# Sliding-window attention and a SiLU MLP: scores in bands of 192 keys from the second group on, in fp32 too, and one tile for the parts of P

## The chip, the cores and the metric

The kernel runs on one core of a Trainium2 chip. The metric is the device time of one execution in microseconds. The kernel before takes 897.84 us, the median of three runs from 897.73 to 897.88.

## The reference

```python
def _attn_ref(q, k, v):                      # 8 batches, 8 heads, 576 tokens, 64 per head
    scores = scale * np.matmul(q, k.transpose(0, 1, 3, 2))
    rel = pos[:, None] - pos[None, :]
    mask = (rel >= 0) & (rel < window)       # window = 128
    scores = np.where(mask, scores + bias[None], -1000000000.0)   # bias = -slope(head) * |rel|
    attn = np.exp(scores - np.max(scores, axis=-1, keepdims=True))
    attn = attn / (np.sum(attn, axis=-1, keepdims=True) + 1e-09)
    return np.matmul(attn, v)

def reference(...):
    x = attn_out.transpose(0, 2, 1, 3).reshape(4608, 512)
    h = x @ w_in                             # 512 x 2048
    g = h * (1.0 / (1.0 + np.exp(-h)))
    return g @ w_out                         # 2048 x 512
```

A query sees itself and the 127 keys in front of it. All inputs and the output are fp32.

## The kernel before

**Attention.** The 4608 tokens are 36 blocks of 128 rows, nine to each pair of batches (a block of index 4 or 5 in such a nine has two batches in it). A *pair* p is half a block: block i = p // 2 and four of its heads (q = p % 2), so there are 72 pairs. In a pair two indices run over the heads: h, the head in the upper or lower 64 partitions of q and k (D = 64), and u, the two such couples. Each pair passes these steps, one function each:

- `scores` (L535, or `scores_banded`, L556): q times k on TensorE into two PSUM banks `sp`, one for each h.
- `other_batch` (L570 to L577): memsets of what belongs to the other batch, on VectorE.
- `row_max` (L588, L598): adds the bias table `tab` (bf16, one table of 256 columns for each head) and finds each row's extreme, on VectorE, four instructions.
- `exps` (L613): exp with the row's extreme as bias, on ScalarE.
- `p_hi`, `p_lo`: P as two fp16 parts: the high part is ScalarE's (L634, L638), the low part VectorE's (L647, L204) or GpSimd's (L202).
- `p_transpose` (L664, L668): DMA transposes, issued by SyncE, into `hl`.
- `attend` (L713): P times v in 24 fp16 matmuls into one PSUM bank `av`, then `normalize` (L726 to L742), `x_hi`, `x_lo` and a transpose to `xt`. Pairs 0 to 7 do this in another way, by transposes on TensorE (L678) and a copy (L687).

A block of queries needs the keys of its own block and of the one before: 256 keys for 128 queries. That is what pairs 0 to 35 compute: `sp[h][:, u]` is 128 x 256, from fp32 q and k, in two matmuls of 128 columns for each u and h (one, where the block is the first of its nine: pairs 18 and 19). Pairs from 36 on are *banded*: the first 64 queries need keys -128 to 63, the second 64 need -64 to 127, so each half of queries takes 192 keys of its own. There the matmuls are on tiles of 64 rows and 64 columns, with q and k as fp16 high and low parts and three terms. For these pairs the first 64 partitions and the second 64 of the bias table are aligned by `rescale_bias` (L371), which at the third and fourth pair of batches moves and scales the table in two instructions, one for each half of the partitions:

```python
for s in range(2):
    off = HALF * s if b == QK16 else 0
    nc.vector.tensor_scalar_mul(tab[halves[s], :, :WIN], tab[halves[s], :, off : off + WIN], ratio[halves[s]])
```

**P's parts.** Pairs 8 to 35 take two tiles `hr` of the pool tag "hr" (two buffers), one for each u, and issue a transpose (128 x 1024) as soon as one u's parts are in. Pairs from 36 on share one persistent tile, `room[0]` (named hr0_0, 64 + 2048 columns, its gaps zeroed once by `clear_room` on GpSimd at position 150): the second half of queries lies 64 columns further left than the first, and two transposes of 64 partitions x 2048 bring the pair into place.

**The MLP.** Nine groups g of 512 tokens, 16 steps n of 128 features each: gemm1 (L1032, L1037; three passes of fp32r in the first group, fp16 later), the activation (`gt` L1065 on ScalarE, `h` L1071 on VectorE, `gh` or `gb` on ScalarE, `gl` L204 or `gb` L1120 on VectorE) and gemm2 (L1248). In the last groups sums of w_in's and w_out's rows shorten the products (L975, L1151).

**What sets the order.** All engines' instructions are issued in program order, written by hand. The program walks through *positions*, one for each half of a gemm step, and `put(point, fn, *a)` enters a function at a position; `at(p)` is the position of pair p's scores: every 8 positions for pairs 0 to 7, the list `CLOSE` for pairs 8 to 15 (which run beside the first group's MLP), every 7 from pair 18 on. At one position, works stand by rank (`rank_of`). PSUM tag "a" has two banks, which scores and av share.

Of the kernel before, what the change touches and what calls it, by code (L numbers as in the profile page):

```python
# [6 lines left out]
F32 = mybir.dt.float32  # L7
# [11 lines left out]
P = 128  # L19
# [55 lines left out]
SUMS, SUMS_STEP = 200, 28  # L75
IN_GAP = 17
HI_SUM, HI_IN = 1, 1
IN_SUMS = tuple(SUMS + SUMS_STEP * j + IN_GAP for j in range(8))
# [3 lines left out]
ALONE_LATE = 4  # L82
X7, X8, X9 = 448, 455, 462
X_SUMS = {(NG - 2, 1): X7, (NG - 1, 0): X8, (NG - 1, 1): X9}
WIN = P + HALF
HR_TAG = "w1_2"
HL_TAG = "w1_3"
ATTEND_BAND = 18
ATTEND_END = 13
HR_CLEAR = 150  # L90
# [5 lines left out]
POOL_FROM = 116  # L96
# [9 lines left out]
ACT_LOW = 1  # L106
V_HI, V_LO = 10, 6
# [10 lines left out]
SUM_TAGS = tuple(f"w1_{k}" for k in range(7, 15))  # L118
# [18 lines left out]
CLOSE = (-6, 5, 8, 14, 20, 26, 32, 38)  # L137
# [15 lines left out]
def tile_window_attention_then_silu_mlp(ctx, tc, qk, v, w_in, w_out, distance, out):  # L153
# [361 lines left out]
    def banded(p):  # L515
        return p >= 2 * QK16 * NBLK
# [24 lines left out]
    def scores_banded(p, flat):  # L541
# [6 lines left out]
        for u in range(2):  # L548
            for both in (first, second):
                for n, (a, b) in enumerate(((0, 0), (1, 0), (0, 1))):  # L550
                    for s, k, keys, at4 in both:
                        if block_of(i) == 0 and k < i:
                            continue
                        for h in range(2):
                            rows = slice(h * D, (h + 1) * D)
                            nc.tensor.matmul(  # L556
                                sp[h][halves[s], u, at4 : at4 + keys.stop - keys.start],
                                q16[i][rows, a, 2 * q + u, halves[s]], k16[k][rows, b, 2 * q + u, keys],
                                start=n == 0, stop=n == 2, skip_group_check=True,
                            )  # L560
# [18 lines left out]
    def row_max(p, k):  # L579
# [4 lines left out]
        if banded(p):  # L584
            for u in range(2):
                if u not in st[p]["t"]:
                    st[p]["t"][u] = pool.tile([P, 2, WIN], F32, tag="t", bufs=3, name=f"t{p}_{u}")
# [6 lines left out]
        for u, h in [(k, 0), (k, 1)] if p < 2 * GT else [(0, k), (1, k)]:  # L594
            if u not in st[p]["t"]:
                tag, bufs = ("x", 4) if 2 * GT < p < 4 * GT and p % 2 and u else ("t", 3)
                st[p]["t"][u] = pool.tile([P, 2, 2 * P], F32, tag=tag, bufs=bufs, name=f"t{p}_{u}")
# [19 lines left out]
    def clear_room():  # L617
        room[0] = r = pool.tile([P, HALF + 16 * P], F16, tag=HR_TAG, bufs=1, name="hr0_0")
# [4 lines left out]
    def split_of(p, u, what):  # L623
        if banded(p):
# [1055 lines left out]
```

## Time and profile before

| | |
|---|---|
| median of three runs | 897.84 us |
| the profiled execution | 896.72 us |
| its span | 894.9 us |
| busy: PE (TensorE) | 886.3 us, 99% |
| busy: DVE (VectorE), ACT (ScalarE), POOL (GpSimd) | 647.4, 589.1, 418.5 us |
| granted TensorE clock | 1.00 in all stretches |

A profile is one execution, with each instruction's start and duration on its engine. PE is the matmuls, PEld the weight loads, which overlap them, SPq SyncE's queue, which issues DMAs. Lnnn is a line of the kernel. A pipelined matmul's row contains its drain, so rows overlap: what an instruction costs its engine is read from the start of one to the start of the next.

### The profile page before, as it was taken

The numbers are of one execution on the slowest core, as the hardware profiler recorded it, in microseconds if no ns is written. First come the engines' busy times: TensorE is split into PE (matmuls) and PEld (weight loads), VectorE is DVE, ScalarE is ACT, GpSimd is POOL, SyncE is SP. The second block draws the span as 40 slices with busy tenths as digits, with TensorE's granted clock in tenths as the row PEclk, the third lists the DMA queues.
The fourth block names the chain that finished last, engine by engine and source line by source line (L and its number), as shares of the span: only waits on it lengthen the run. The fifth ranks groups of instructions, "written<-read, shape, count | busy, mean of one in ns | idle before, by whom it ended". The sixth has DMA issues, their size and how long they took to land.

```text
span 894.9 us, 22095 instructions
## 1 busy us (share of the span) xinstructions
PE 886.3 (99%) x8617; PEld 589.6 (66%) x8617; DVE 647.4 (72%) x1654; ACT 589.1 (66%) x1321; POOL 418.5 (47%) x494
## 2 busy tenths in 40 slices
PE   9999999999999999999999999999999999999998
PEld 7877777888855555445455554445555568899997
DVE  6997988678876766655777667575776659776665
ACT  7789987776578855777765555565566554465653
POOL 2356651112112211666676776686777412443441
PEclk9999999999999999999999999999999999999999
DMA  8979925345588744869885557565575455400000
GB/s 322 399 191 263 244 56 134 72 95 96 117 216 220 191 96 119 179 163 225 188 155 108 109 105 154 123 118 109 125 166 95 84 85 142 142 26 13 14 25 26
DMA packets 207193, 123.22 MB, mean 138 GB/s; under 512 B 170864, under 2 KB 173040, under 8 KB 207088
## 3 DMA queue, kind: packets, MB, share of 16 engines
q1 hardware_dynamic: 206656, 121.41, 56.7%
q8 instruction: 68, 1.11, 0.5%
q10 hardware_dynamic: 432, 0.39, 0.1%
q14 instruction: 37, 0.30, 0.1%
HBM read 66.72 MB, written 13.63 MB: 90 GB/s over the span
## 4 chain that ended last, share of the span: by engine, by line
PE 79%; DVE 8%; ACT 5%; DMA 3%; POOL 3%; issue 2%; SPq 1%; DVEq 0%; POOLq 0%; ACTq 0%
PE o L1248 26%; PE h L1032 22%; PE m L1151 7%; PE h L1037 5%; PE sp L535 4%; PE av L713 4%; PE h L975 3%; PE hb L975 3%; PE sp L556 2%; PE av L699 1%; ACT t L613 1%; DMA qs<-qk 1%; SPq L664 1%; DMA vm<-v 1%; PE pt L678 1%
## 5 line engine op out<-in xcount | busy, mean ns | idle before, releaser
L1032 PE MATMUL h<-xt,w 128*128 128x512 f16 (+1 forms) x1344 | 269.0, 349 | 0.0
L1248 PE MATMUL o<-w,gb 128*128 128x512 f16 x960 | 224.4, 379 | 0.8 <-DVE gb L1120 0.6
L1032 PEld LDWEIGHTS <-w 128*128 128x128 f16 x1344 | 126.6, 98 | 111.7 <-issue 3.3
L1071 DVE SCALAR_TENSOR_TENSOR h<-gt,h 128x512 f32<-128x512 f32 x112 | 77.6, 693 | 127.2 <-ACT gt L1065 126.6
L1248 PEld LDWEIGHTS <-gb 128*128 128x128 f16 x960 | 90.2, 98 | 104.9 <-DVE gb L1120 2.6
L1065 ACT ACTIVATE gt<-h,tsc 128x512 f32<-128x512 f32 x104 | 71.1, 683 | 112.7 <-PE h L1032 105.2
L202 POOL TENSOR_TENSOR hr<-t,hr 128x384 f16<-128x384 f32 (+2 forms) x54 | 55.9, 1036 | 127.7 <-ACT hr L634 64.4
L202 POOL TENSOR_TENSOR x<-xs,x 128x256 f16<-128x256 f32 x54 | 37.3, 690 | 160.3 <-ACT x L752 151.1
L1248 PE MATMUL o<-w,gh 128*128 128x512 f32 x256 | 82.9, 405 | 0.1
L1106 ACT ACTIVATE gb<-h 128x512 f16<-128x512 f32 x80 | 47.4, 592 | 35.5 <-DVE h L1071 35.2
L613 ACT ACTIVATE t<-t,mx,vsc 128x192 f32<-128x192 f32 x144 | 69.0, 537 | 1.2
L1120 DVE SCALAR_TENSOR_TENSOR gb<-h,gb 128x512 f16<-128x512 f32 x80 | 54.8, 685 | 18.7 <-ACT gb L1106 18.6
L613 ACT ACTIVATE t<-t,mx 128x256 f32<-128x256 f32 (+1 forms) x144 | 61.8, 488 | 3.6 <-DVE mx L598 2.7
L713 PEld LDWEIGHTS <-hl 128*128 128x128 f16 x1464 | 51.8, 98 | 14.6 <-issue 3.9
L713 PE MATMUL av<-v,hl 128*128 128x65 f16 (+1 forms) x1464 | 54.9, 193 | 0.1
L1083 POOL TENSOR_TENSOR gt<-gt 128x256 f32<-128x256 f32 x27 | 21.4, 794 | 68.5 <-DVE gt L1074 68.5
L1248 PEld LDWEIGHTS o<-w,gh 128*128 128x128 f32 x256 | 45.6, 188 | 10.0 <-issue 0.5
L598 DVE CUSTOM_DVE_ANT_0 t<-sp,tab 128x256 f32<-128x256 f32 (+1 forms) x144 | 50.1, 402 | 1.9 <-PE sp L535 1.7
L1248 PE MATMUL o<-w,gl 128*128 128x512 f32 x128 | 50.7, 396 | 0.2
L980 ACT COPY hs<-h 128x128 f32<-128x128 f32 x72 | 19.0, 264 | 41.7 <-PE h L975 38.9
L204 DVE SCALAR_TENSOR_TENSOR hr<-t,hr 128x384 f16<-128x384 f32 (+2 forms) x54 | 42.8, 792 | 5.0 <-ACT hr L634 3.8
L202 POOL TENSOR_TENSOR w<-wm,w 128x512 fp32r<-128x512 f32 x32 | 43.7, 1366 | 2.5
(236 smaller groups left out, 1835.2 us busy)
## 6 DMA issues: line engine op xcount, KB each, us to landing
qs<-qk SPq DMA_DIRECT2D x18, 512.0 KB, 4.6
r<-qk SPq DMA_DIRECT2D x18, 512.0 KB, 4.5
wr<-w_in SPq DMA_DIRECT2D x16, 512.0 KB, 6.5
wr<-w_out SPq DMA_DIRECT2D x16, 512.0 KB, 6.2
rv<-v SPq DMA_DIRECT2D x30, 256.0 KB, 3.6
out<-ot SPq DMA_DIRECT2D x28, 256.0 KB, 2.4
vm<-v SPq DMA_DIRECT2D x27, 256.0 KB, 4.4
q<-qk SPq DMA_DIRECT2D x18, 256.0 KB, 3.4
```

Of the source, the lines that this page charges most:

```text
L202: engine.tensor_sub(out, a, b)
L598: nc.vector.tensor_tensor_reduce(out=st[p]["t"][u][:, h, 2 * P - n :], in0=st[p]["sp"][h][:, u, o].rearrange("p o c -> p (o c)"), in1=tab[ ...
L613: nc.scalar.activation(x, x, AF.Exp, bias=mx[:, 2 * u + h : 2 * u + h + 1], scale=scale)
L713: nc.tensor.matmul(av[:, 2 * u + h, : rhs.shape[-1]], lhs, rhs, start=(n == 0), stop=(n == len(seq) - 1), skip_group_check=True,)
L975: nc.tensor.matmul(h[to], w_of(j, w, a, cc), x_of(g, t, x, b, cc), start=w in ("11", "S1") and i == 0, stop=i == len(terms) - 1, skip_grou ...
L1032: nc.tensor.matmul(o, w[:, wp, cc], x, start=start and k == 0, stop=stop, skip_group_check=True)
L1065: nc.scalar.activation(gt, hps[n], AF.Tanh, scale=scale)
L1071: nc.vector.scalar_tensor_tensor(out=h, in0=gt, scalar=1.0, in1=h, op0=ALU.add, op1=ALU.mult)
L1106: nc.scalar.activation(gh, gt, AF.Copy, scale=cut_of(n))
L1120: nc.vector.scalar_tensor_tensor(out=gl, in0=gt, scalar=cut_of(n), in1=f32(gh) if n // NF < OUT16 else gh, op0=ALU.mult, op1=ALU.subtract)
L1151: nc.tensor.matmul(product(k), a[:, k], sum_part(k, j, part), start=j == 0 and side == 0 and a is gh and part == 0, stop=n == last and a i ...
L1248: nc.tensor.matmul(ops[ti], a[:, t], w, start=(f == 0 and i == 0), stop=(f == NF - 1 and i == len(seq) - 1), skip_group_check=True,)
```

## The change

- `banded` holds from pair 8 on. Pairs 8 to 35 keep fp32 q and k and one term: 16 matmuls (8 of 128 columns, 8 of 64) instead of 8 of 128; pairs 18 and 19 get 8 instead of 4. Row max, exps and parts of these pairs have 192 columns for each head instead of 256.
- `shift_bias`, new, aligns the second half of the bias table once, at position -16, so `rescale_bias` is one instruction.
- All pairs from 8 on use the one room, cleared at position -18; `p_transpose` is called once for a pair, when both u are in. gemm1's sums `hsum` become one tile of the tag "hr".
- Positions and tags move: pairs 10 to 13 one or two positions later (`CLOSE`), av8, av9 and av10 to 15 at 17, 13 and 14 behind their scores (before 17, 12, 15), pair 8's parts at position 4, v's conversion one position later, sums of w_out's rows from 172 in steps of 25 (before 200 and 28), constants of the last groups by one or two (`X8`, `X9`, `POOL_FROM`, `ALONE_LATE`).

The core of the diff:

```diff
-SUMS, SUMS_STEP = 200, 28
-IN_GAP = 17
+SUMS, SUMS_STEP = 172, 25
+IN_GAP, IN_ONE = 16, 131
-HR_CLEAR = 150
+HR_CLEAR = -18
+SHIFT = -16
-POOL_FROM = 116
+POOL_FROM = 114
-CLOSE = (-6, 5, 8, 14, 20, 26, 32, 38)
+CLOSE = (-6, 5, 10, 15, 21, 27, 32, 38)
+LATE9, LATE10 = 0, 0
+P8 = (4, 4)
+A8, A9, A10 = 17, 13, 14
...
-        for s in range(2):
-            off = HALF * s if b == QK16 else 0
-            nc.vector.tensor_scalar_mul(
-                tab[halves[s], :, :WIN], tab[halves[s], :, off : off + WIN], ratio[halves[s]]
-            )
+        nc.vector.tensor_scalar_mul(tab[:, :, :WIN], tab[:, :, :WIN], ratio)
+
+    def shift_bias():
+        nc.vector.tensor_copy(tab[halves[1], :, :WIN], tab[halves[1], :, HALF:])
...
     def banded(p):
-        return p >= 2 * QK16 * NBLK
+        return p >= 2 * GT
...
-                for n, (a, b) in enumerate(((0, 0), (1, 0), (0, 1))):
+                terms = ((0, 0), (1, 0), (0, 1)) if i >= QK16 * NBLK else ((None, None),)
+                for n, (a, b) in enumerate(terms):
                     for s, k, keys, at4 in both:
...
+                            lhs = qs[i][rows, 2 * q + u, halves[s]] if a is None else q16[i][rows, a, 2 * q + u, halves[s]]
+                            rhs = ks[k][rows, 2 * q + u, keys] if a is None else k16[k][rows, b, 2 * q + u, keys]
...
-    def p_transpose(p, u):
...
-        nc.sync.dma_start_transpose(hl[:, : 4 * n], hr[:, : 4 * n * P])
+    def p_transpose(p):
+        tag, bufs = ("hl", 2)
+        if ATTEND_BAND > 12 and p >= LONG_FROM and p % 3 == 2:
+            tag, bufs = HL_TAGS.get(p, HL_TAG), 1
+        both = pool.tile([P, 2, 8, P], F16, tag=tag, bufs=bufs, name=f"hl{p}")
+        st[p]["hl"] = {u: both[:, u] for u in range(2)}
+        for s in range(2):
+            off = HALF * (1 - s)
+            nc.sync.dma_start_transpose(
+                both.rearrange("p u a c -> p (u a) c")[:, :, halves[s]], room[0][halves[s], off : off + 16 * P]
+            )
...
-            late = 2 * (p == 2 * GT + 2)
+            late = {2 * GT + 1: LATE9, 2 * GT + 2: LATE10}.get(p, 0)
...
-                put(n + 4 + late + u * (1 + more), p_transpose, p, u)
+            put(n + 5 + late + more, p_transpose, p)
```

Where the order of instructions changes:

On TensorE, the scores of pair 10 (`sp10`) against gemm2 of the first group (`o0`) and av8. Before:

```order
L1037 MATMUL h2_776<-xh_71,w0_2_648 128x512
L535 MATMUL sp10_0_799<-k4_387,q5_499 128x128
L535 MATMUL sp10_1_800<-k4_387,q5_499 128x128
...
L1248 MATMUL o0_3_751<-w1_1_697,gl1_739 128x512
L1037 MATMUL h3_859<-xh_71,w0_3_745 128x512
L1037 MATMUL h3_859<-xl_72,w0_3_745 128x512
L1037 MATMUL h3_859<-xh_71,w0_3_745 128x512 x2
L1037 MATMUL h3_859<-xl_72,w0_3_745 128x512
L1037 MATMUL h3_859<-xh_71,w0_3_745 128x512
L713 LDWEIGHTS hl8_765
```

and in the change:

```order
L1238 MATMUL o0_3_774<-w1_1_709,gl1_762 128x512
L563 MATMUL sp10_0_849<-k4_387,q5_499 64x128
L563 MATMUL sp10_1_850<-k4_387,q5_499 64x128
L563 MATMUL sp10_0_849<-k5_501,q5_499 64x128
L563 MATMUL sp10_1_850<-k5_501,q5_499 64x128
L563 MATMUL sp10_0_849<-k5_501,q5_499 64x64
...
L1026 MATMUL h3_871<-xh_71,w0_3_768 128x512
L1026 MATMUL h3_871<-xl_72,w0_3_768 128x512
L1026 MATMUL h3_871<-xh_71,w0_3_768 128x512 x2
L1026 MATMUL h3_871<-xl_72,w0_3_768 128x512
L1026 MATMUL h3_871<-xh_71,w0_3_768 128x512
L700 LDWEIGHTS hl8_727
```

Between pair 10's scores and av8 there stood twelve matmuls of gemm2 and six of gemm1, and now six of gemm1 alone.

On VectorE, at the same place, pair 10's row max (`t10`), pair 9's low parts (`hr` from `t9`), `wm4` and `gl2`. Before:

```order
L577 MEMSET sp10_1_800 128x2x64
L598 ISA t10_0_830,mx10_809<-sp10_0_799,tab_67 128x256
L598 ISA mx10_809 128x1
...
L647 SCALAR_TENSOR_TENSOR hr9_0_813<-t9_0_757,hr9_0_813 128x512
L1296 SCALAR_TENSOR_TENSOR wm4_0_825<-wm4_0_825,wr4_0_392 128x512
L204 SCALAR_TENSOR_TENSOR gl2_837<-h2_776,gh2_836 128x512
L647 SCALAR_TENSOR_TENSOR hr9_1_839<-t9_1_759,hr9_1_839 128x512
```

and in the change:

```order
L642 SCALAR_TENSOR_TENSOR hr0_0_528<-t9_0_780,hr0_0_528 128x2x192
L1286 SCALAR_TENSOR_TENSOR wm4_0_831<-wm4_0_831,wr4_0_392 128x512
L209 SCALAR_TENSOR_TENSOR gl2_835<-h2_794,gh2_834 128x512
L576 MEMSET sp10_0_849 64x2x64
L576 MEMSET sp10_1_850 64x2x64
L595 ISA t10_0_883,mx10_867<-sp10_0_849,tab_67 128x192
...
L642 SCALAR_TENSOR_TENSOR hr0_0_528<-t9_1_782,hr0_0_528 128x2x192
```

Pair 9's first low part, `wm4` and `gl2` stood behind the row max and now stand ahead of it.

On VectorE, the place of `shift_bias` (L377 COPY) in the change, where nothing stood before between `hl7` and the next row of `vmx0`:

```order
L271 TENSOR_REDUCE vmx0_523<-early2_230 128x1
L675 COPY hl7_536<-pt7_1_538 128x512
L377 COPY tab_67<-tab_67 64x8x192
L271 TENSOR_REDUCE vmx0_523<-early3_278 128x1
L713 TENSOR_SCALAR r6_557<-av6_547 128x4
```

The four rows around the copy have kept their order.

## Rows read from the trace of the kernel before

**Rows 1.** The page, parts 1 and 4; TensorE's waits: us, times, longest.

```profile
PE 886.3 (99%) x8617; PEld 589.6 (66%) x8617; DVE 647.4 (72%) x1654; ACT 589.1 (66%) x1321; POOL 418.5 (47%) x494
...
PE 79%; DVE 8%; ACT 5%; DMA 3%; POOL 3%; issue 2%; SPq 1%; DVEq 0%; POOLq 0%; ACTq 0%
...
PE warm L224 <- POOL ident masks.py:199: 1.3, 1, 1.3
...
PE pt L678 <- ACT t L613: 0.3, 1, 0.3
```

**Rows 2.** Timeline of TensorE around a pair's scores: start us, us, instruction.

```profile
285.75 0.59 PE L1032 MATMUL h<-xt,w 128*128 128x512 f16 x2
286.27 1.16 PE L535 MATMUL sp<-k,q 64*128 64x128 f32 x16
287.36 0.82 PE L1032 MATMUL h<-xt,w 128*128 128x512 f16 x3
```

**Rows 3.** Lines L535 and L556: ns of one, min/median/max, first and last start.

```profile
L535 PEld LDWEIGHTS sp<-k,q x544: 182/188/188, 4.8 to 342.9; 64*128 64x128 f32 x182
L535 PE MATMUL sp<-k,q x544: 272/272/373, 4.8 to 343.0; 64*128 64x128 f32 x182
...
L556 PEld LDWEIGHTS <-packed x1632: 102/107/110, 354.4 to 728.4; 64*64 64x64 f16 x182
```

**Rows 4.** Timeline of TensorE around a pair of the later groups.

```profile
481.67 1.03 PE L1032 MATMUL h<-xt,w 128*128 128x512 f16 x4
482.62 0.24 PE L556 MATMUL sp<-packed 64*64 64x128 f16 x2
482.63 0.24 PE L556 MATMUL sp<-packed,packed 64*64 64x128 f16 x2
...
482.82 0.19 PE L556 MATMUL sp<-packed 64*64 64x64 f16 x2
...
482.91 0.22 PE L556 MATMUL sp<-packed,packed 64*64 64x128 f16 x2
...
483.27 1.04 PE L1032 MATMUL h<-xt,w 128*128 128x512 f16 x4
```

**Rows 5.** Groups by line and form on ScalarE: busy us, mean ns | idle before.

```profile
L634 ACT CAST hr<-t 128x384 f16<-128x384 f32 x72 | 34.5, 502 | 8.0 <-DMA hl<-hr 7.9
L638 ACT ACTIVATE hr<-t 128x512 f16<-128x512 f32 x52 | 31.4, 620 | 2.1 <-DMA hl<-hr 2.1
```

**Rows 6.** Busy us (instructions) from 75 to 85 us: PE, PEld, DVE, ACT, POOL; clock, DMA.

```profile
75.00:85.00 10.00, 10.00 (x75) 7.91 (x74) 7.76 (x21) 10.00 (x27) 5.83 (x7) 1.00 1.07 269
```

**Rows 7.** Timelines of VectorE and of TensorE near 33 us; line L371.

```profile
33.33 0.42 DVE L742 TENSOR_TENSOR early<-av,r 128x256 f32<-128x256 f32 x1
...
32.65 1.81 PE L767 MATMUL xp<-ident,early 128*128 128x128 f32 x15
...
L371 DVE TENSOR_SCALAR tab<-tab,vsc x4: 607/792/1419, 352.7 to 546.7; 64x1536 bf16<-64x1536 bf16 x4
```

**Rows 8.** Timelines of VectorE, then of TensorE, 53 to 60 us.

```profile
53.37 0.42 DVE L598 CUSTOM_DVE_ANT_0 t<-sp,tab 128x256 f32<-128x256 f32 x1
...
55.61 0.68 DVE L204 SCALAR_TENSOR_TENSOR gl<-h,gh 128x512 fp32r<-128x512 f32 x1
...
54.11 0.90 PE L713 MATMUL av<-v,hl 128*128 128x65 f16 x24
...
56.78 0.39 PE L1248 MATMUL o<-w,gl 128*128 128x512 f32 x1
...
59.16 1.28 PE L535 MATMUL sp<-k,q 64*128 64x128 f32 x14
```

**Rows 9.** SyncE near 449 us, landings of L664, ScalarE near 60 us.

```profile
449.49 3.21 SPq L664 DMA_TRANSPOSE hl<-hr  x2
...
DMA to landing us min/median/max: 3.6/4.2/5.8
...
60.48 0.63 ACT L638 ACTIVATE hr<-t 128x512 f16<-128x512 f32 x1
```

More of the change, by code (lines that the diff above doesn't have):

```diff
@@ L105 @@
 ACT_LATE = 6
-ACT_LOW = 1
-V_HI, V_LO = 10, 6
+ACT_LOW = 2
+SUM_LATE = 2
+V_HI, V_LO = 9, 5
 IN_HI16, IN_LO16 = (9, 8), (6, 4)
@@ L617, in clear_room @@
     def clear_room():
-        room[0] = r = pool.tile([P, HALF + 16 * P], F16, tag=HR_TAG, bufs=1, name="hr0_0")
+        room[0] = r = pool.tile([P, HALF + 16 * P], F16, tag="hr", bufs=1, name="hr0_0")
         gaps = r[:, : 16 * P].rearrange("p (a c) -> p a c", a=8)
@@ L621, in clear_room, with split_of @@
         nc.gpsimd.memset(r[:, 16 * P :], 0.0)
-    def split_of(p, u, what):
-        if banded(p):
-            parts = what[:, HALF:].rearrange("p (u a h c) -> p u a h c", u=2, a=2, h=2)
-            return parts[:, u, :, :, :WIN]
-        n = 2 - blocks(p).start
-        return what[:, : 4 * n * P].rearrange("p (a h c) -> p a h c", a=2, h=2)
-    def p_hi(p, u):
-        t, n = st[p]["t"][u], (2 - blocks(p).start) * P
-        if banded(p):
-            st[p]["hr", u] = hr = room[0]
-            nc.scalar.copy(split_of(p, u, hr)[:, 0], t)
-            return
-        st[p]["hr", u] = hr = pool.tile([P, 8 * P], F16, tag="hr", bufs=2, name=f"hr{p}_{u}")
+    def split_of(u):
+        parts = room[0][:, HALF:].rearrange("p (u a h c) -> p u a h c", u=2, a=2, h=2)
+        return parts[:, u, :, :, :WIN]
@@ L646, in p_lo @@
             return
         nc.vector.scalar_tensor_tensor(
-            out=hr[:, 1], in0=t[:, :, 2 * P - n :], scalar=PSCALE, in1=hr[:, 0], op0=ALU.mult, op1=ALU.subtract
+            out=hr[:, 1], in0=t, scalar=PSCALE, in1=hr[:, 0], op0=ALU.mult, op1=ALU.subtract
         )
-    def p_transpose(p, u):
-        n = 2 - blocks(p).start
-        hr = st[p].pop(("hr", u))
-        if u == 0:
-            tag, bufs = (HL_TAG, 1) if banded(p) and p % 3 == 2 and ATTEND_BAND > 12 else ("hl", 2)
-            st[p]["both"] = pool.tile([P, 2, 8, P], F16, tag=tag, bufs=bufs, name=f"hl{p}")
-        both = st[p]["both"]
-        st[p]["hl"][u] = hl = both[:, u]
-        if banded(p):
-            if u == 0:
-                return
-            for s in range(2):
-                off = HALF * (1 - s)
-                nc.sync.dma_start_transpose(
-                    both.rearrange("p u a c -> p (u a) c")[:, :, halves[s]], hr[halves[s], off : off + 16 * P]
-                )
-            return
-        nc.sync.dma_start_transpose(hl[:, : 4 * n], hr[:, : 4 * n * P])
+    def p_transpose(p):
[9 more added lines that the diff above has]
+            )
@@ L969, in gemm1_seven @@
             hps[n] = [ps_of("h", f"h{n}"), ps_of("wy"[n % 2], f"hb{n}")]
-            hsum[n] = pool.tile([P, 4, P], F32, tag="hr", bufs=2, name=f"hs{n}")
+            if not hsum:
+                hsum["all"] = pool.tile([P, 2, 4, P], F32, tag="hr", bufs=1, name="hs")
+            hsum[n] = hsum["all"][:, n % 2]
         h = [a[:, k * P : (k + 1) * P] for a in hps[n] for k in range(2)]
```

60 lines of the change are left out of this document (30 added, 30 removed).

## The prediction

> **What bounds the kernel now.** I read the page first, to see which engine is short of time: TensorE is busy for 886.3 of 894.9 us, and 79% of the chain that ended last is its work [rows 1]. Then the list of what TensorE waited for: its five groups run from 1.3 us, at the start, to 0.3, and come to 3.3 in all [rows 1]. So every microsecond taken off TensorE's own work shortens the run, and every wait that a change puts in front of TensorE lengthens it. VectorE and ScalarE have room over the whole span, but not everywhere, and this is the second thing to read, in the busy time by stretch: from 75 to 85 us ScalarE has no gap [rows 6]. A change that takes work off all engines and adds waits in that stage must be costed there. All durations are from the profiled execution, which took 896.72 us; the median of the runs shown is 897.84, 1.12 more, and I add that at the end.
>
> **Scores in bands (pairs 8 to 35).** This is the gain. Before, a pair's scores are 8 fp32 matmuls of 128 columns, in the trace two records each, 16 in all. From the row before to the row behind, a pair between fp16 matmuls occupies 287.36 - 285.75 = 1.61 us, in which two neighbours of 0.21 to 0.22 lie (two of them take 0.59, four 1.03), so 1.18 [rows 2, 4]. The 16 records span 1.16 us, of which the longest record, 0.373, is the drain of the last [rows 2, 3]; the 0.79 in front of it are 7 steps of 0.113 us, two records of the two row halves together in each step. Eight steps are 0.90 us of streaming, 512 columns at 1.75 ns, and 1.18 - 0.90 = 0.28 are entry and exit.
>
> After, each of the two u has two sets of four matmuls: 128 columns and 64 columns, on 64x64 tiles, so 2 x 192 = 384 columns pass. The nearest row for such tiles is the fp16 pair of the later groups: three sets of four with 128 columns lie between 482.62 and 482.82, 0.07 us each, and three with 64 between 482.82 and 482.91, 0.03 each, so there the short set does take half, and the four tiles do work together [rows 4]. That pair occupies 483.27 - 481.67 = 1.60 less four neighbours of 0.21, 0.74, of which two u of 0.29 are streaming, so its entry and exit are 0.16. For the fp32 pair I get 384 x 1.75 = 0.67 of streaming. With the fp32 pair's own entry it is 0.95, a gain of 0.23; with the fp16 pair's, 0.83, a gain of 0.35. The weights of these matmuls stay fp32 (a weight load of 182 to 188 ns, against 102 to 110 in fp16 [rows 3]), so the fp32 end is the nearer one: I take 0.25. At the other end, if a 64-column set costs 0.075 a step rather than 0.056, the gain is 0.15. Of the 28 pairs, 18 and 19 have only their own block: 4 matmuls of 128 columns become 4 of 128 and 4 of 64, which I cost at nothing. 26 x 0.25 = **-6.5 us** (-3.9 to -9.1).
>
> **The other engines' share.** A part of P falls from 620 to 502 ns on ScalarE [rows 5], and a row max on VectorE has a quarter fewer columns. None of this is on the path by itself; it is slack for VectorE and ScalarE in the crowded stage and I cost it at nothing.
>
> **The copy that shifts the bias table.** It stands in VectorE's queue just behind hl7's copy. From 29.2 us on VectorE runs there without a gap, to the end of the last L742 at 33.75, and TensorE's transposes of `early` (from 32.65) need that result: the copy is on the path in full [rows 7]. The nearest row is the later rescaling of the same table, 64 x 1536 bf16 in place too: 607 to 1419 ns, median 792 [rows 7]. I take **+0.8** (0 if TensorE has slack there that I don't see, at most 1.4). The Trainium skill (VectorE: DVE Perf Modes, "The perf-mode tier table") gives `tensor_copy` and a `tensor_scalar` of bf16 in SBUF the same top rate, 693 ns for 2048 elements; by it the copy would be about 0.5 us, an estimate, and the sum 0.3 lower. Rescaling later in one instruction instead of two halves removes two VectorE instructions off the path: nothing.
>
> **Pair 10's row max is now behind av8's turn.** The PSUM tag "a" has two buffers, shared by scores and P x V, so av8 can start only when half of pair 10's row max is done. Before, that half ended at 53.37 + 0.42 = 53.79, and av8 started at 54.11 [rows 8], without waiting. In the new order P's low part of pair 9, wm4 and gl2, which ran behind the row max (gl2, the third, from 55.61 for 0.68), stand ahead of it, at about 0.6 us each, since one begins before the row of the other ends. 53.79 + 1.8 less two shorter row maxima is 55.5; less 0.3 for pair 8's low parts, which VectorE has done earlier now, 55.2. TensorE, 0.25 faster here, is at av8 at 53.9. I take **+1.3** (0 to 2). In return pair 11's scores come a position later, and the 0.3 us by which they are stretched at 59.16 (14 records in 1.28 us, against 16 in 1.16) should go: **-0.3** [rows 8].
>
> **One tile for P's parts.** Before, a pair up to 35 has two tiles and a transpose for each as it is ready; now the second transposes of a pair must have landed before ScalarE may write the next pair's parts. Two transposes of the one tile take, in the later groups, 3.21 us to issue, and each lands 4.2 us behind its issue (at most 5.8), so I reckon 5.5 us from the first issue to the last landing [rows 9]. Pairs lie 5 or 6 positions apart in group 0; a position there is 1.68 us (av8, at 54.11, stands at 11 in the order of before, pair 11's scores, at 59.16, at 14 [rows 8]), so 8.4 or 10 us. From a pair's first part to its last low part pass about 3.5 us, so the room is free again 9 us behind its first use: even, with ScalarE busy throughout [rows 6]. In the later groups, where pairs lie further apart, ScalarE waited 7.9 us in all at this very place, and none of TensorE's waits names it [rows 5, 1]. The worst is pair 10: pair 9's low part ends at about 57.2, its transposes land at some 63, and ScalarE, which comes to pair 10's part at 60.48, stands for 2 us [rows 9]; gt, gh and so gl behind it are late by up to that. Such an operand may have little to spare (gl2 ends at 55.61 + 0.68 = 56.29 and is read at 56.78 [rows 8]), while ScalarE wins back 0.24 us a pair [rows 5]. I take **+0.5** (0 to 4).
>
> **What moves at no cost.** hsum as one tile, the new tags, the sums of w_out's rows on GpSimd earlier and denser, two sums from VectorE to GpSimd near the end: TensorE's waits in the trace are small ones [rows 1], of which some may go and others appear. I cost them at 0 (-1 to +1).
>
> **Sum:** -6.5 + 0.8 + 1.3 - 0.3 + 0.5 = -4.2, so 892.5 for a profiled execution, and **893.6 us** for the median. A difference of under 0.2% (1.8 us) is about what cannot be told from no change here.
>
> **Rivals.**
> 1. *No new wait shows:* av8 and the room cost nothing, -6.5 + 0.8 - 0.3 = -6.0, so 891.8. For it: ScalarE's parts of P are 0.24 us a pair shorter in the crowded stage [rows 5, 6]. Against it: the order at av8.
> 2. *The room becomes the bound of group 0:* ScalarE loses 1 to 2 us at pairs 10, 11, 12 and 14, where the spacing is 5 positions or the queue of transposes is late, and what gl has to spare is used up after the first. With 1 us each that is +4 instead of +0.5: 897.1, no change.
> 3. *The weight loads set the pace (slower):* a fp32 matmul loads its weights for each of its two passes, and 16 matmuls have twice the loads of 8. If a load, not a column, is what a step costs, the eight sets' steps keep 0.113 whatever their width: no gain, and the other terms remain: +2.3, 900.1. It decides where a fp32 load of a 64x64 tile is over 0.05 us in the stream. For it: 64 columns need half the time, the load does not; against: fp16's short sets at 0.03.
> 4. *Column halves in turn (slower):* the row halves run together in fp32, but no fp32 row shows two column halves at once. If the two halves of queries go one behind the other, a pair streams 2 x (2 x 0.226 + 2 x 0.113) = 1.36 instead of 0.90: +0.45 x 26 = 11.7, with the other terms 910.7, and 911.8 for the median. The fp16 pair speaks against it, whose two halves of a set begin at 482.62 and 482.63 [rows 4]. The Trainium skill (TensorE: Matmul & The Clock Gate, Part 3, "The mechanism") has it that a weight load overlaps running matmuls only where the row group differs, and here both column halves share one. By that rule this rival would hold; rows 4, where four tiles of two row groups overlap, don't agree with it for fp16.
>
> **How the numbers follow.** Forecast 58% (its own range 891.2 to 896.2: the score term between 0.15 and 0.33 a pair, and av8's); rival 1 16%; rival 2 15%; rival 3 6%; rival 4 5%. Faster by over 0.2% means under 896.0: nearly all of the forecast, rival 1 and a little of rival 2, 0.75. Within 0.2%: the rest of rival 2, 0.14. Slower: rivals 3 and 4, 0.11. The range leaves out rivals 3 and 4 and the far ends: 889.8 (0.33 a pair and no new wait) to 898.0 (rival 2).
>
> **What would show it.** A banded fp32 pair occupying 0.9 to 1.0 us instead of 1.18, with 32 records; 1.13 or more says rival 3, 1.5 or more rival 4. VectorE without a gap from 29 to 34.7 us with the copy in it, and `early`'s transposes later by its length. A gap of TensorE just ahead of av8 near 55 us, ended by the row max. ScalarE waiting for the transposes at pairs 10 to 15, and gaps of TensorE at gl's matmuls between 60 and 100 us: none over 0.5 us says rival 1, several of a microsecond rival 2. The prediction is wrong as a whole if TensorE's busy time does not fall by 4 us or more.

## The result, and the profile after

The change makes the kernel slower: 907.34 us (median of six runs, 905.37 to 909.21) against 897.79 us (six runs, 896.87 to 898.41), a ratio of 1.0106 with a 95% interval of 1.009 to 1.0123. The forecast was 893.6 us, with a range up to 898.0. The runs of the change also lie further apart, 3.8 us against 1.5.

| | before | after |
|---|---|---|
| the profiled execution, its span | 896.72, 894.9 us | 909.21, 907.3 us |
| busy: TensorE | 886.3 us, 99% | 883.9 us, 97% |
| busy: VectorE, ScalarE, GpSimd | 647.4, 589.1, 418.5 us | 627.8, 579.4, 415.4 us |
| mean granted TensorE clock | 1.000 | 0.996 |

Every engine has less to do, and the span is 12.4 us longer: the time went into waits, and into two stretches of a lower clock that came behind such waits. The profiled execution of the change is the slowest of its six, 1.9 us above their median. Parts 1 and 4 of the changed kernel's page, and the first four of 15 groups of TensorE's waits (us, times, longest), against [rows 1]:

```profile
PE 883.9 (97%) x9049; PEld 585.0 (64%) x9049; DVE 627.8 (69%) x1655; ACT 579.4 (64%) x1321; POOL 415.4 (46%) x500
...
PE 72%; DMA 7%; DVE 7%; ACT 6%; POOL 3%; SPq 2%; issue 2%; DVEq 0%; ACTq 0%; POOLq 0%
...
PE av L700 <- DVE mx L595: 5.0, 5, 2.3
PE o L1238 <- ACT gb L1096: 2.7, 2, 1.9
PE hb L964 <- DMA wy<-away: 2.3, 2, 1.2
PE sp L563 <- DVE xs L729: 1.6, 2, 0.8
```

TensorE's share of the chain fell from 79% to 72%, that of DMA rose from 3% to 7%. The first three groups name three places, and each has its experiments below.

**The bands came out as forecast.** The changed kernel's timeline of TensorE around a pair between fp16 matmuls, then line L563 (ns, min/median/max, first and last start), against [rows 2, 3]:

```profile
252.47 2.76 PE L1021 MATMUL h<-xt,w 128*128 128x512 f16 x12
255.17 0.90 PE L563 MATMUL sp<-k,q 64*64 64x128 f32 x32
256.00 2.76 PE L1021 MATMUL h<-xt,w 128*128 128x512 f16 x12
...
L563 PEld LDWEIGHTS sp<-k,q x864: 129/133/136, 35.4 to 345.7; 64*64 64x64 f32 x173
```

From the start of the scores to the start of the next matmul pass 0.83 us, before 287.36 - 286.27 = 1.09: 0.26 a pair, where 0.25 was reckoned. All four tiles of a set work together in fp32 too: 32 records pass in 0.90 us, and the first four of this pair start within 0.02 us (255.17 to 255.19). An fp32 weight load of a 64x64 tile takes 133 ns instead of 188.

**The copy** takes 0.56 us on VectorE, and TensorE's transposes then wait 0.25 us for `early`, against [rows 7]:

```profile
31.25 0.56 DVE L377 COPY tab<-tab 64x1536 bf16<-64x1536 bf16 x1
...
34.66 0.77 PE L754 MATMUL xp<-ident,early 128*128 128x128 f32 x5 [0.25 <-DVE early L729]
```

**The first group.** The changed kernel's timelines of ScalarE, VectorE and TensorE from 82 to 91 us, one row behind the other:

```profile
82.85 0.53 ACT L635 ACTIVATE hr<-t 128x384 f16<-128x384 f32 x1 [0.90 <-DMA hl<-hr]
...
83.41 0.56 DVE L642 SCALAR_TENSOR_TENSOR hr<-t,hr 128x384 f16<-128x384 f32 x1 [0.69 <-ACT hr L635]
...
88.66 0.58 DVE L209 SCALAR_TENSOR_TENSOR x<-xs,x 128x256 f16<-128x256 f32 x1 [1.66 <-ACT x L739]
...
89.77 0.34 DVE L595 CUSTOM_DVE_ANT_0 t<-sp,tab 128x192 f32<-128x192 f32 x1
...
90.55 0.88 PE L700 MATMUL av<-v,hl 128*128 128x65 f16 x24 [2.27 <-DVE mx L595]
```

ScalarE comes to a pair's high part and waits 0.90 us for the transposes of the pair before, which still read the room. VectorE's low part waits for ScalarE, x's low part 1.7 us for ScalarE's x, and the row max, which stands behind them in VectorE's queue, begins at 89.77. TensorE is at av by 88.3 and stands 2.27 us, until half of the row max has read one of the two banks of tag "a". The waits from 45 to 110 us, first two lines of the change, then one of the kernel before:

```profile
ACT hr L635 <- DMA hl<-hr: 4.2, 4, 1.3
PE av L700 <- DVE mx L595: 4.2, 4, 2.3
...
ACT hr L638 <- DMA hl<-hr: 2.1, 2, 1.7
```

ScalarE's four waits are at the parts of pairs 10, 11, 12 and 14 (1.29, 0.87, 0.90 and 1.14 us). Before, ScalarE waited 2.1 us there and TensorE not at all; from 75 to 85 us TensorE was busy without a gap [rows 6].

**From 404 to 420 us.** The changed kernel's timelines of SyncE's queue, ScalarE, VectorE and TensorE:

```profile
404.89 3.20 SPq L654 DMA_TRANSPOSE hl<-hr  x2
408.13 2.40 SPq L855 DMA_DIRECT2D away<-wx  x2
410.57 0.44 SPq L280 DMA_DIRECT2D qs<-qk  x1
...
411.55 0.52 ACT L635 ACTIVATE hr<-t 128x384 f16<-128x384 f32 x1 [1.74 <-DMA hl<-hr]
415.16 0.63 ACT L289 ACTIVATE qs<-qs 128x512 f32<-128x512 f32 x1 [3.09 <-DMA qs<-qk]
...
416.33 0.56 DVE L209 SCALAR_TENSOR_TENSOR hr<-t,hr 128x384 f16<-128x384 f32 x1 [5.88 <-ACT hr L635]
...
419.51 2.46 PE L1238 MATMUL o<-w,gb 128*128 128x512 f16 x6 [1.88 <-ACT gb L1096]
```

and the same place in the kernel before, SyncE's queue and ScalarE:

```profile
397.69 3.17 SPq L664 DMA_TRANSPOSE hl<-hr  x2
400.90 1.18 SPq L275 DMA_DIRECT2D qs<-qk  x1
...
404.00 1.31 SPq L868 DMA_DIRECT2D away<-wx  x2
...
405.88 0.63 ACT L284 ACTIVATE qs<-qs 128x512 f32<-128x512 f32 x1 [2.05 <-DMA qs<-qk]
```

Behind the two transposes the kernel before issues the load of qs, and later `away`, which writes finished sums of w_in's rows to memory. In the change, whose sums stand elsewhere, `away` is ahead of qs: it takes 2.40 us to issue, qs follows at 410.57, and ScalarE waits 3.09 us for it where it waited 2.05. The second high part of P, gt, gb and gemm2 stand behind that wait, TensorE for 1.88 us. Near 363 us another `away` is ahead of the load of vm (SyncE's queue, then ScalarE):

```profile
363.19 0.90 SPq L855 DMA_DIRECT2D away<-wx  x2
364.13 0.46 SPq L260 DMA_DIRECT2D vm<-v  x1
...
369.98 0.63 ACT L274 ACTIVATE vm<-vm 128x512 f32<-128x512 f32 x1 [3.46 <-DMA vm<-v]
```

Here the write takes only 0.90 us to issue, but the load behind it lands 5.8 us after its own issue, where the same load before took 3.5. ScalarE's wait for vm is 3.46 us, where it had none.

**The clock behind two waits.** Before, the granted clock is 1.00 to the end of TensorE's work. In the change two stretches differ (length; busy us of PE, PEld, DVE, ACT, POOL; then clock, DMA share, GB/s):

```profile
420.00:424.00 4.00, 3.88 (x32) 2.26 (x32) 2.48 (x11) 3.01 (x9) 3.57 (x5) 0.57 0.92 198
785.00:790.00 5.00, 4.36 (x36) 3.60 (x37) 1.87 (x3) 2.45 (x6) 1.09 (x1) 0.66 0.79 262
```

From 421 to 423 and from 786 to 789 us the clock is 0.50, the lower of its two levels (1.2 instead of 2.4 GHz). TensorE had stood 1.88 us up to 419.51, and 1.23 and 1.07 us between 783.1 and 785.64, with two matmuls between them. At the lower level av's 24 matmuls take 1.33 us to the start of the next (421.76 to 423.09), at full clock 0.71 (90.55 to 91.26). Of full clock 4 x 0.43 + 5 x 0.34 = 3.4 us are missing in these rows, an estimate of what the two stretches cost this execution beside the waits. Not every such wait is followed by one: behind the 2.27 us up to 90.55 the clock stays 1.00, and so it does in the run with the sums moved back behind its wait for wy.

Where does the delay build up? Both kernels have the same gemm matmuls, so the start of the same one can be compared: the change is 4.0 us behind at 107 us, 1.1 behind at 277 (the bands' gain), 3.6 behind at 373, 10.8 at 424, 8.9 at 754, and 12.4 at the end of this execution. The 10.8 and what follows contain the 1.7 us of lower clock near 422, and the end the 1.7 near 787.

### The profile page after: what moved, and what is told of

Read it like the earlier page. It is cut to its first block, busy times and chain, and to the rows that moved or that the text cites. A ratio compares the mean times of both kernels' runs of the same rounds, so it can differ in the third digit from the quotient of the medians.

```text
span 907.3 us, 23001 instructions
## 1 busy us (share of the span) xinstructions
PE 883.9 (97%) x9049; PEld 585.0 (64%) x9049; DVE 627.8 (69%) x1655; ACT 579.4 (64%) x1321; POOL 415.4 (46%) x500
## 3 DMA queue, kind: packets, MB, share of 16 engines
q8 instruction: 71, 1.16, 0.5%
## 4 chain that ended last, share of the span: by engine, by line
PE 72%; DMA 7%; DVE 7%; ACT 6%; POOL 3%; SPq 2%; issue 2%; DVEq 0%; ACTq 0%; POOLq 0%
PE o L1238 24%; PE h L1021 21%; PE m L1141 7%; PE av L700 4%; PE sp L563 3%; PE h L964 3%; PE h L1026 3%; PE hb L964 3%; DMA hl<-hr 3%; DMA vm<-v 2%; SPq L654 2%; DMA qs<-qk 2%; ACT gt L1054 1%; PE h L993 1%; PE av L687 1%
## 5 line engine op out<-in xcount | busy, mean ns | idle before, releaser
L207 POOL TENSOR_TENSOR hr<-t,hr 128x384 f16<-128x384 f32 x54 | 51.4, 951 | 131.5 <-ACT hr L635 131.5
L207 POOL TENSOR_TENSOR x<-xs,x 128x256 f16<-128x256 f32 x54 | 39.2, 726 | 156.1 <-ACT x L739 150.3
L595 DVE CUSTOM_DVE_ANT_0 t<-sp,tab 128x192 f32<-128x192 f32 x256 | 75.4, 348 | 1.6 <-PE sp L563 1.6
L635 ACT ACTIVATE hr<-t 128x384 f16<-128x384 f32 x128 | 63.0, 512 | 12.1 <-DMA hl<-hr 12.1
L700 PEld LDWEIGHTS <-hl 128*128 128x128 f16 x1464 | 52.5, 98 | 21.4 <-issue 10.8
L1073 POOL TENSOR_TENSOR gt<-gt 128x256 f32<-128x256 f32 x29 | 24.3, 837 | 77.1 <-DVE gt L1063 77.1
L619 ACT ACTIVATE t<-t,mx 128x192 f32<-128x192 f32 (+2 forms) x144 | 56.6, 452 | 4.4 <-DVE mx L595 3.1
L209 DVE SCALAR_TENSOR_TENSOR hr<-t,hr 128x384 f16<-128x384 f32 x54 | 39.9, 738 | 10.2 <-ACT hr L635 10.1
L1296 POOL CAST w<-wm 128x512 fp32r<-128x512 f32 x32 | 19.6, 611 | 56.3 <-DVE wm L1286 35.4
```

The costliest lines, as they stand in the source:

```text
L207: engine.tensor_sub(out, a, b)
L595: nc.vector.tensor_tensor_reduce(out=st[p]["t"][u][:, k], in0=st[p]["sp"][k][:, u], in1=tab[:, 4 * q + 2 * u + k, :WIN], scale=scale, scal ...
L619: nc.scalar.activation(x, x, AF.Exp, bias=mx[:, 2 * u + h : 2 * u + h + 1], scale=scale)
L635: nc.scalar.activation(split_of(u)[:, 0], st[p]["t"][u], AF.Copy, scale=scale)
L700: nc.tensor.matmul(av[:, 2 * u + h, : rhs.shape[-1]], lhs, rhs, start=(n == 0), stop=(n == len(seq) - 1), skip_group_check=True,)
```

## The experiments

The theory: the bands pay, and three side effects cost more. (1) The sums' new positions put writes ahead of loads in SyncE's queue. (2) The single room makes ScalarE wait, and through VectorE's order TensorE. (3) The constants of the last groups cost something near 785 us. The rivals: GpSimd's denser sums rather than the queue; the room in place of the sums also in the later stage; the order of instructions in place of the room in the first group; and that the bands were worth nothing.

The runs came in four sets, each with the kernel before beside it. Its medians were 897.40 us (the first four experiments), 898.30 (the room in the first group, the writes, three and four edits), 897.65 (the sums in the kernel before, the constants alone, v, plain scores with four edits) and 897.41 (the early loads), and 897.79 beside the change. A price taken between runs of two sets is uncertain by up to 0.9 us.

### The shift on GpSimd

```diff
-        nc.vector.tensor_copy(tab[halves[1], :, :WIN], tab[halves[1], :, HALF:])
+        nc.gpsimd.tensor_copy(tab[halves[1], :, :WIN], tab[halves[1], :, HALF:])
```

> The changed kernel with one edit: the bias table's shift is a GpSimd copy, not a VectorE one. In the profile of the change TensorE's gemm1 of the first group starts 0.6 us later than before (36.19 against 35.59 us). Theory that the copy is on the path: that start comes back to about 35.6, and the run is 0.5 to 0.8 us shorter than the change's 907.3. Rival, that something else makes it late (the clearing of the room, the first banded scores): no difference. If GpSimd's copy takes over 3 us and the first banded row max waits for it, the start is later still.

Measured: 907.72 us (905.70 to 909.04), the change's own time. GpSimd needs 1.46 us for the copy, but gemm1 starts only 0.18 us earlier than in the change. The transposes of `early` are no longer stretched (1.84 us to the start of the scores, 2.56 in the change and 1.85 before), but TensorE's work ahead of them is already 0.53 us later than in the change at 28.9 us, for a reason that was not looked for. The copy is no large part of the loss.

### The sums at the positions of before

```diff
-SUMS, SUMS_STEP = 172, 25
-IN_GAP, IN_ONE = 16, 131
+SUMS, SUMS_STEP = 200, 28
+IN_GAP = 17
-IN_SUMS = (IN_ONE,) + tuple(SUMS + SUMS_STEP * j + IN_GAP for j in range(7))
+IN_SUMS = tuple(SUMS + SUMS_STEP * j + IN_GAP for j in range(8))
```

> The changed kernel with the positions of the sums of w_in's and w_out's rows as before (200 and 28, gap 17, no early one). In the change TensorE loses 2.7 us near 370 and 4.0 us from 410 to 424, where a write of such sums (away) stands ahead of the load of qs in SyncE's queue. Theory that the sums' new places make these losses: 4 to 6 us less, about 902. Rival, that the room does it (the transposes, and ScalarE behind them): within 1 us of the change.

Measured: 901.88 us (901.55 to 903.32), 5.5 less than the change. Against the change the same matmul is 7.5 us earlier at 421 us and 5.6 at 748. This is the largest part of the loss. Of the lead by profile some 1.7 us are the clock, since this run's trace has no stretch of lower clock near 422.

### A second room in the later stage

```diff
+MORE_CLEAR, ROOMS_FROM = 150, 31
+    def clear_more():
+        room[1] = r = pool.tile([P, HALF + 16 * P], F16, tag="w1_2", bufs=1, name="hr0_1")
...
+    def room_of(p):
+        return room[p % 2 if p >= ROOMS_FROM else 0]
```

> The changed kernel with a second room (in the tag that the room had before) from position 150, taken in turn by the pairs from 31 on. ScalarE waits there for the transposes 3.0 us in 3 between 350 and 450 us and more later. Theory that the room makes the losses near 370 and 410 to 424: 4 to 6 us less, about 902. Rival (the sums' places): those waits of ScalarE go to nearly nothing, and the time stays within 1 us.

Measured: 906.71 us (906.07 to 910.11), no gain. ScalarE's waits of the changed kernel between 355 and 430 us, and then of this one:

```profile
ACT vm L274 <- DMA vm<-v: 6.6, 3, 3.5
ACT qs L289 <- DMA qs<-qk: 3.1, 1, 3.1
ACT hr L635 <- DMA hl<-hr: 2.8, 2, 1.7
```

```profile
ACT vm L275 <- DMA vm<-v: 6.4, 3, 3.1
ACT qs L290 <- DMA qs<-qk: 4.2, 1, 4.2
```

The wait for the transposes is gone from the list, and the waits for vm and qs stay. In this stage the room is not what costs; the rival that puts the loss there falls.

### Plain scores in the changed kernel

```diff
+        if 2 * GT <= p < 2 * QK16 * NBLK and block_of(i):
+            for u in range(2):
+                for o in range(blocks(p).start, 2):
+                    for h in range(2):
...
+                            sp[h][:, u, 1 - o], qs[i][rows, 2 * q + u], ks[i - 1 + o][rows, 2 * q + u],
```

> The changed kernel, but the scores of pairs 8 to 35 (without 18 and 19) are again 8 fp32 matmuls of 128 columns, whose results lie elsewhere in the bank, so that the rest works on other numbers: the output is not the reference's. It prices the bands on TensorE alone. By the rows (1.18 us a pair before, 0.91 in the change) 26 pairs are 7 us: 914 if all of it reaches the end, and less if the waits swallow a part of it. If the gain was never there, 907.

Measured: 909.60 us (908.40 to 910.19), only 2.3 more. The same matmul is 4.4 us later at 311 us, where 23 pairs at 0.26 us make 6.0, 2.6 later at 400, 0.3 at 423 and 0.9 from 460 us on. Waits had swallowed part of the gain by 400; the 1.7 us lost between 400 and 460 are as much as the change's own stretch of lower clock there, which this run doesn't have. The bands pay, but only a part of what they win on TensorE arrives.

### A second room in the first group

```diff
+MORE_CLEAR, ROOM_ONE = -17, (9, 11, 13)
+    def clear_more():
+        room[1] = r = pool.tile([P, HALF + 16 * P], F16, tag="big", bufs=2, name="hr0_1")
...
+    def room_of(p):
+        return room[1 if p in ROOM_ONE else 0]
```

> The changed kernel with a second room for P's parts in the first group: pairs 9, 11 and 13 use a buffer of the tag big that is idle there. In the change ScalarE waits 4.2 us in 4 for the transposes between 45 and 110 us, VectorE's low parts wait 4.4 us for ScalarE, the row max stands behind them, and TensorE waits 4.2 us at av, which needs a bank that the row max has to read. Theory that this chain starts at the single room: TensorE's waits at av between 60 and 95 us fall from 4.2 us to under 1, and the run is 3 to 4 us shorter than the change (907.3). Rival, that the order of the instructions on VectorE does it (row max behind low parts and wm): ScalarE's waits go, av's stay at 3 us or more.

Measured: 904.66 us (902.35 to 905.31), 2.7 less. TensorE's waits of this kernel between 45 and 110 us:

```profile
PE av L710 <- DVE mx L596: 1.0, 2, 0.8
```

ScalarE has no wait for the transposes left there, and TensorE's at av fall from 4.2 us to 1.0. The order of VectorE's instructions is unchanged in this run, so the room starts the chain. Counted from the kernel before beside each run (9.55 and 6.36 us more), the gain is 3.2 us, about what was expected. In the profiled executions the lead is 3.2 us at 88 us, 3.5 at 280, 2.4 at 314 and 2.1 at 751; this run has a stretch of lower clock of its own from 287 to 290 us, behind a wait of 1.65 us.

### The writes two positions later

```diff
-IN_AWAY = 7
+IN_AWAY = 9
```

> The changed kernel with one number: the writes of the sums (away) are issued two positions later, so that in SyncE's queue they stand behind the loads of vm and qs that they stood ahead of near 363 and 408 us. The sums themselves stay where the change has them. Theory that the queue's order makes the loss near 370 and from 410 to 424: ScalarE's waits for vm and qs fall from 9.7 us to the 5 of the run with the sums moved back, and the time to 902 to 903. Rival, that GpSimd's denser sums or the transfers' own traffic make it: 906 to 908.

Measured: 905.06 us (904.93 to 906.66), 2.3 less, between the two predictions. This kernel's SyncE queue:

```profile
401.77 3.18 SPq L654 DMA_TRANSPOSE hl<-hr  x2
404.99 1.27 SPq L280 DMA_DIRECT2D qs<-qk  x1
406.30 0.94 SPq L855 DMA_DIRECT2D away<-wx  x2
```

qs now follows the transposes. ScalarE's waits for vm and qs between 355 and 430 us:

```profile
ACT vm L274 <- DMA vm<-v: 2.9, 3, 1.9
ACT qs L289 <- DMA qs<-qk: 2.0, 1, 2.0
```

They fall from 9.7 to 4.9 us, to just what they are with the sums moved back (4.1 and 0.8), as the theory asks; but the time falls by 2.3 us and not by 5.5. In the profiled executions this run is 6.2 us ahead of the change at 417 us and 3.7 at 750, against 5.6 for the sums moved back; both leads contain the 1.7 us of the change's lower clock near 422. The queue's order is thus shown to cost the waits for vm and qs, and 2.3 of the median's 5.5 us. The rest, some 3 us, stays open: where the sums themselves and their traffic fall was not taken apart.

### The sums of the change in the kernel before

```diff
-SUMS, SUMS_STEP = 200, 28
+SUMS, SUMS_STEP = 172, 25
```

(with the gap, the first position and the tags' order of the change)

> The kernel before with the sums of w_in's and w_out's rows at the change's positions (172 and 25, gap 16, the first at 131, the tags in the change's order), and nothing else of the change. Theory that these positions cost by themselves, through the writes that stand ahead of the loads of vm and qs: 4 to 6 us slower than before, and ScalarE's waits for vm and qs between 355 and 430 us at 9 or more, where before has 5.5. Rival, that they cost only together with the single room or a TensorE that comes earlier: within 1 us of before.

Measured: 904.08 us (903.01 to 904.55) against 897.65 for the kernel before beside it, a ratio of 1.0075 (1.006 to 1.009): 6.4 us from these positions alone. SyncE's queue and ScalarE in this run:

```profile
403.96 1.57 SPq L868 DMA_DIRECT2D away<-wx  x2
405.57 0.44 SPq L275 DMA_DIRECT2D qs<-qk  x1
...
410.43 0.63 ACT L284 ACTIVATE qs<-qs 128x512 f32<-128x512 f32 x1 [3.63 <-DMA qs<-qk]
```

The same write ahead of the same load, and a wait of 3.63 us. It needs neither the room nor the bands. ScalarE's waits for vm and qs came to 5.7 us in all, not to 9, and before they were 5.5: the expectation was right on the time and wrong on that sum. Most of the loss arises between 380 and 440 us (by profile 1.5 us at 380, 7.1 at 440), but these waits in sum don't show why.

### The constants of the last groups, alone

```diff
-ALONE_LATE = 5
-X7, X8, X9 = 448, 456, 464
-POOL_FROM = 114
+ALONE_LATE = 4
+X7, X8, X9 = 448, 455, 462
+POOL_FROM = 116
```

> The changed kernel with the constants of the last groups alone as before (sums of x at 455 and 462, late activation 4, two sums on VectorE again). On the three edits together they gave 2.1 us. Theory that this part is separate: 2 us less than the change (905.3), and the waits for wy near 785 from 2.3 us to 0.6. Rival, that it only pays where the rest is early: 907.

Measured: 906.07 us (902.70 to 906.50), 1.3 less than the change with overlapping runs: inconclusive alone. TensorE's waits for wy fall from 2.3 us to 0.7, as the theory asks.

### Three edits, and four

The sums' positions of before, the second room of the first group and the shift on GpSimd:

> Three edits together: the sums' positions of before, the second room of the first group, the shift on GpSimd. If the losses are separate, they add: 907.3 - 5.5 - 3.5 - 0.4 = 898, level with before. If the delay won in the first group is swallowed later, as most of the 7 us of the plain scores were, about 901.

Measured: 897.72 us (895.19 to 901.06), a ratio to before of 0.9994 (0.9981 to 1.0006): level with before, as the separate losses add up to. With the constants of the last groups too:

> The three edits, and the constants of the last groups as before too (the sums of x in 455 and 462, the late activation 4, two sums on VectorE again). In the change TensorE waits 2.3 us near 785 for the sums that come back from memory (wy), before 0.6. Theory that the constants make it: 1 to 2 us less than the three edits alone. Rival, that these waits come from the whole run's delay or from the writes: the same time.

Measured: 895.60 us (893.69 to 896.91), 0.9967 (0.9955 to 0.998). TensorE's wait for wy in it, against 2.3 us in the change:

```profile
PE hb L974 <- DMA wy<-away: 0.5, 1, 0.5
```

In the run with three edits it was 2.2, so the constants are worth about 2 us here, 1.7 of it this wait; which of them was not tried apart. With v's conversion a position earlier, as before (`V_HI, V_LO = 10, 6`):

> All four edits, and v's conversion a position earlier, as before. With it the sums, the tail and v stand where before has them, and only the first group's positions, the room, the bands and the shift on GpSimd are left of the change. If v's place matters, TensorE's wait at av for v (0.4 us) goes and the time is 0.4 us or more below 895.6; otherwise the same.

Measured: 894.47 us (894.06 to 895.95), 0.997 (0.996 to 0.998) of before. TensorE's wait for v is still 0.4 us, and against the kernel before beside each the two runs are the same (0.997 and 0.9967): the 1.1 us between their medians are not shown to be a gain.

### Plain scores with the four edits

> All four edits, and the scores of pairs 8 to 35 (without 18 and 19) as 8 fp32 matmuls of 128 columns again, with results that lie elsewhere in the bank, so that the output is not the reference's. In the change the same step cost 2.3 us of the 7 that TensorE spends more. Theory that waits swallow the gain of the bands, and that fewer waits let more of it through: 4 to 7 us slower than the four edits (895.6). Rival, that the stage from 350 to 430 us, whose loads have a pace of their own, swallows it whatever comes ahead: 2 to 3 us slower.

Measured: 897.21 us (895.78 to 898.32), 1.6 more than with bands, and 2.7 more than the run with v moved, which was taken beside it: nearer to the rival of this run. Against the four edits the bands' lead is 4.2 us at 262 us, 2.7 at 398 and 1.0 at 436, and stays there. Between 355 and 440 us something has a pace of its own.

### The loads ahead of the transposes

```diff
-            put(n, vscale_load, b, i)
-            put(n + 1, qk_load, b, i)
+            put(n - 4 * (b == 3), vscale_load, b, i)
+            put(n + 1 - 4 * (b == 3), qk_load, b, i)
```

> The edits of the run with v's conversion moved back (894.5, against 897.7 before), and the loads of vm and qs for the fourth pair of batches (nine of each, between 355 and 440 us) issued four positions earlier, so that they stand ahead of the pair's transposes in SyncE's queue and not behind them. Up to 300 us that run is 4 to 5 us ahead of one with plain scores, at 437 us only 1. Theory that in this stage the pace is set by a ring (transposes, the loads behind them in the queue, ScalarE's wait for the loads, the next pair's parts, its transposes): ScalarE's waits for vm and qs there fall from 6 us to under 2, the lead stays, and the time falls by 2 to 3 us, to about 892. Rival, that the transfers themselves are short of bandwidth there: no gain, 894 to 896.

Measured: 892.85 us (892.24 to 893.85), 0.9949 (0.9933 to 0.9966) of before, 1.6 less than without the early loads. SyncE's queue in this run, and its only wait of ScalarE for a DMA between 355 and 430 us:

```profile
397.85 1.09 SPq L261 DMA_DIRECT2D vm<-v  x1
399.05 0.38 SPq L281 DMA_DIRECT2D qs<-qk  x1
...
403.73 3.40 SPq L664 DMA_TRANSPOSE hl<-hr  x2
...
ACT hr L645 <- DMA hl<-hr: 0.9, 2, 0.5
```

ScalarE's 6 us of waits for vm and qs are gone: the loads lie ahead of the transposes. TensorE's only wait from 380 to 450 us, in the run with v moved, in the run with four edits and plain scores, and in this run:

```profile
PE o L1248 <- DVE gb L1120: 1.7, 1, 1.7
PE o L1260 <- DVE gb L1132: 0.3, 1, 0.3
PE o L1248 <- DVE gb L1120: 0.3, 1, 0.3
```

With bands TensorE came to gb 1.7 us early and had to wait; the early loads end that. With plain scores:

> The same with the scores of pairs 8 to 35 (without 18 and 19) as 8 fp32 matmuls of 128 columns, whose results lie elsewhere in the bank: the output is not the reference's. If the ring swallowed the bands' gain, this is now 4 us or more behind the run beside it; if something else swallows it, 1 to 2 us, as without the early loads.

Measured: 896.23 us (895.32 to 897.89), 3.4 more than with bands, where without the early loads it was 1.6 to 2.7; in the traces the bands' lead from 440 us on is 3.0 us, where it was 1.0 (1.8 against the run with v moved). That is short of the 4 us or more which the theory asked for: the ring swallowed a part, some 0.7 to 2 us. Another part of the lead is lost at 285 to 316 us (from 4.2 to 2.2, and 3.0 from 400 on); that place was not tried. And in the kernel before:

> The kernel before with the same loads four positions earlier and nothing else. Its waits for vm and qs are 5.5 us between 355 and 430 us, and TensorE waits there 0.7 and 0.8 us. Theory of the ring: up to 1.5 us faster than before (896); not slower. Rival: no difference, or slower where the loads take the bandwidth of others.

Measured: 895.72 us (895.14 to 895.95), 0.9976 (0.9967 to 0.9985) of before. The kernel before, with plain scores, gains 1.7 us from the same edit: the loads' place cost there too, though none of TensorE's longer waits named it. On that footing the bands and the room, with the side effects that were found undone, are worth 895.72 - 892.85 = 2.9 us, not 6.5.

## Why the prediction was wrong, point by point

The forecast was 4.2 us less and the median moved by 9.5 more, 13.7 us apart. The step that failed most is the term "what moves at no cost", put at 0 (-1 to +1): in it the sums' positions measured 5.5 us and the constants of the last groups about 2. The score term returned 2.3 of its 6.5 us, and the room cost 2.7 us instead of 0.5. These come to 13.9; prices taken one at a time overlap, since a delay is partly swallowed by the stage behind it.

- **Scores, -6.5: right on TensorE (0.26 us a pair, some 7 us), wrong at the end.** Taking the scores back cost 2.3 us in the change, 1.6 to 2.7 with four edits, 3.4 with the loads early too. The step that failed here is "every microsecond taken off TensorE's own work shortens the run": the rows showed where TensorE waited, not how close the loads were behind it. The loads' ring is shown to have swallowed a part; where the rest of the 7 us went stays open. (A slip in the sum, on which nothing hangs: with 0.33 a pair and the other terms as they stand the forecast's own lower end is 891.6, not 891.2.)
- **The sign that it set itself, TensorE's busy time down by 4 us or more, failed too:** 886.3 to 883.9, 2.4 less. The bands' part is there: in the two runs with early loads, which have no such stretches of lower clock, it is 878.8 us with bands and 885.4 with plain scores, 6.6 apart. In the change the two stretches give back some 3.4 us (the estimate above), since matmuls take longer in them. The prediction had no term for the clock.
- **The sums, 0 (-1 to +1): this is the step that made the sign of the result wrong.** They cost 5.5 us in the change and 6.4 in the kernel before. I looked at GpSimd, which makes the sums, and at TensorE's small waits, but not at SyncE's queue, where the writes were moved past the loads of vm and qs. That order is shown to cost 2.3 us; what makes the other 3 is open.
- **One room, +0.5 (0 to 4): the place was right, the size too small.** The second room gives 2.7 us (3.2 counted from the kernel before). The chain that I wrote (gt, gh, gl) is not the one that came: it went through VectorE's low parts, and the row max behind them, to av's bank. Rival 2 had the room as the bound, at just the pairs 10, 11, 12 and 14, with about 1 us of ScalarE at each, and put it at 4 us.
- **av8 and the row max, +1.3: found at pairs further on.** At av8 the trace has 0.23 us of idle time (0.4 counted from start to start); the same wait, for a bank that the row max holds, came to 4.2 us over the group, most of it with the room as its start. The -0.3 for pair 11's stretched scores came true: 1.40 us to the next matmul before, 0.83 now, as at other pairs.
- **The copy, +0.8:** 0.56 us, and nothing at the end when it is taken off VectorE. The Trainium skill (VectorE: DVE Perf Modes, "The perf-mode tier table") had led to an estimate of about 0.5 us, and the trace agrees.
- **The constants of the last groups, 0:** about 2 us with the other losses undone, 1.3 us and unclear alone.
- **Rivals 3 and 4** named TensorE as the cause and gave 900 and 912 us; the measured time lies between them, for another reason. By the rule of the Trainium skill (TensorE: Matmul & The Clock Gate, Part 3, "The mechanism"), that a weight load overlaps running matmuls only where the row group differs, the two column halves would have gone one behind the other; 32 records in 0.90 us don't agree with it.

## What to carry to other kernels

When a table of positions moves work, look at every queue that its instructions pass, the DMA queue's order first: a write that nobody waits for cost its issue time here (up to 2.40 us) to the load behind it, and the engine that waits in order for that load carries it on. A shared buffer is priced by what stands behind its waiter in order on two engines, not by the waiter's own slack. And an engine that is 99% busy can still be followed by a ring of loads that is only just fast enough: take the price of a saving from a run that gives it back, at the end and not at its place. Before prices are read from two traces, compare the granted clock in them: here some 1.7 us between two profiles were the clock alone.

## What the runs showed that I had not expected

- Four fp32 matmuls on 64x64 tiles, two column halves and two row halves, run together: 32 records in 0.90 us, where 16 on 64x128 took 1.16. Those weight loads take 133 ns, not 188.
- The same copy of 64 x 1536 bf16 takes 0.56 us on VectorE and 1.46 us on GpSimd.
- Two writes of 256 KB each took 2.40 and 1.57 us to issue right behind two transposes, 0.94 and 1.31 us where they stood further back in the queue. Over all kept traces, 58 such pairs right behind P's transposes took 1.51 to 3.78 us (median 1.65), and 78 elsewhere 0.84 to 2.79 (median 0.91).
- Waits of TensorE of 1.9 and 2.3 us were followed by stretches in which the granted clock stood at its lower level, at a price of about 1.7 us each on top of the wait (an estimate from the clock in the rows); a wait of the same length elsewhere was not.
